# Weighted-value matmuls of an attention slot dealt out between feed-forward matmuls (slots 9 to 31)

## The chip, the cores and the metric

The kernel runs on one core of one Trainium2 chip. The metric is the device time of one execution in microseconds (us). The engines are written as the profile writes them: PE (TensorE, matmuls), PEld (its weight loads), DVE (VectorE), ACT (ScalarE), POOL (GpSimd), SP (SyncE). Each engine works through its own list of instructions in order.

## The reference

Attention with a relative position bias feeds a bilinear feed-forward layer. Cut to what matters:

```python
# q, k, v: (8, 8, 576, 64): batch, heads, positions, head size
scores = scale * q @ k.T + bias            # bias depends on head and on |i - j|
attn   = exp(scores - max) ; attn = attn / (sum(attn) + 1e-9)
x      = (attn @ v)  -> (8 * 576, 512)     # the heads of a position side by side
out    = ((x @ w_a) * (x @ w_b)) @ w_out   # w_a, w_b: 512 x 1536; w_out: 1536 x 512
```

"Weighted values" are the product attn @ v. The kernel divides by the sum of a row only after that product: v carries a column of ones, so the same matmuls give the sums.

## The kernel before

**Pairs and slots.** Two heads of one batch make a pair p, and there are 32 pairs, four to a batch. After a written-out opening (pairs 0 to 7 and the first feed-forward work), a loop over s = 8 to 32 (from line 868) treats one pair in each "slot" s: it computes the scores and exponentials of pair s, the weighted values of pair s - 1, and a fixed quota of feed-forward work on tokens that were finished long before. The slot is a Python list of steps, `steps`, and the order of the steps is the order in which the instructions stand on every engine: the kernel places them by hand (`manual_schedule`). The framework adds the semaphores, one for each read of something that another engine writes and for each buffer that is used again.

**Scores.** `qk(s, 0)` and `qk(s, 2)` are two pairs of score tiles of 128 x 1024 (line 415), each from four 512-column matmuls on half the rows of the array. `ex` (ACT, line 439) takes the exponential into a bfloat16 tile `at`, out of a pool of ten. `mul` (DVE, line 444) multiplies it by the bias table. The last 64 positions have tiles of their own: `qk(s, 2)` adds eight 64-column matmuls into the tiles `trb` and `qr` (line 424), `qk_tail` makes `qkt`, `ex_tail` and `mul_tail` (line 531) finish the tile `att`. `qr` is a tile of the pool `ps_av`, which has one buffer.

**Weighted values.** `av(p, jqs)` is `av_mm` and then `av_norm`. `av_mm(p, (0, 1, 2))` takes the same single buffer of `ps_av` and puts 27 matmuls into it: for each of three blocks of 128 positions one of 130 columns (line 568) and eight of 65 columns (line 578). `av_mm(p, (3, 4))` is the second block of 14: one of 130 and eight of 65, then five of 130 columns for the last 64 positions (lines 568 and 572). Each of them has a weight load of its own, since the attention tile is the stationary operand. `av_norm` runs on DVE: the reciprocal of the sums (line 589), a multiplication into the tile `XG` (line 591), and for the second block two small ones (line 596). After the second block `t_x` sends two DMA transposes from SP, which bring `XG` into `xn`, the feed-forward input (lines 604 and 607).

**Feed-forward.** A unit is four 512-column matmuls: `ff_a` (tile pa, then a copy by ACT, line 649), `ff_b` (tile pb, then DVE's product `g`, line 652), both through `ff_in` (line 642), or a third of an output tile po (`ff_o_mm`, line 679). A chunk of 512 tokens is 24 units of pa and pb in turn and then 12 of po. pa, pb and po share two PSUM buffers. In the list of steps each "unit" stands for one such unit, nine to a slot.

**Order of a slot before.** With U for a unit, a slot with s % 4 of 1, 2 or 3 reads:

```
qk(s,0) ex0 | U ex1 AV(0,1,2) U mul0 U mul1 | v_next qk(s,2) ex2 ex_rows U ex3 U mul2 mul_rows |
AV(3,4) t_x U | U mul3 | qk_tail ex_tail U U mul_tail
```

In slots with s % 4 = 0 ("fourth slots": 12, 16, 20, 24 and 28 among those that the change touches) the part AV(3,4) t_x U and one more U stand before v_next and qk(s,2), so that the last pair of a batch is ready for the next slot's feed-forward. Slot 8 has no weighted values. Slot 32 has no new pair: it starts with AV(0,1,2) and goes on with units.

Of the kernel before, what the change touches and what calls it, by code (L numbers as in the profile page):

```python
# [13 lines left out]
def kernel(  # L14
# [11 lines left out]
    nc = tc.nc  # L26
    FP32 = mybir.dt.float32
# [4 lines left out]
    B, H, S, Dh = 8, 8, 576, 64  # L32
# [18 lines left out]
    ps_av = ctx.enter_context(tc.tile_pool(name="ps_av", bufs=1, space=bass.MemoryType.PSUM))  # L51
# [192 lines left out]
    def warm_up(n, dst=None):  # L244
        for _ in range(n):
# [7 lines left out]
                     start=True, stop=True)  # L253
# [154 lines left out]
    def qk(p, t0, ts=None):  # L408
        qT, kT, _ = operands(p)
        st[p].setdefault("at", [None] * NM)  # L410
        for t in ts or (t0, t0 + 1):
            ps = ps_sc.tile([128, 2, 512], FP32, tag="sc", name=f"qk{p}_{t}")
            for hh in range(2):
                r = slice(64 * hh, 64 * hh + 64)
                nc.tensor.matmul(out=ps[:, hh, :], lhsT=kT[r, t, :], rhs=qT[r, :, :],  # L415
                                 start=True, stop=True)
            st[p]["ps", t] = ps
        if shared(p) and t0 == 2:
            z = operands(p)[2]
            rows = (trb.bitcast(FP32), ps_av.tile([128, 512], FP32, tag="av", name=f"qr{p}"))  # L420
            for t in range(NM):
                for hh in range(2):
                    r = slice(64 * hh, 64 * hh + 64)
                    nc.tensor.matmul(out=rows[hh][:, ST * t:ST * t + ST], lhsT=kT[r, t, :],  # L424
                                     rhs=z[r, 0, ST * hh:ST * hh + ST], start=True, stop=True)
            st[p]["rows"] = rows

    def ex_rows(p):
        st[p]["att"] = at = att[p % 2]
        for hh in (1, 0):  # L430
            nc.scalar.activation(
                out=at[:, 0:512].rearrange("p (t h c) -> p h t c", h=2, t=NM)[:, hh, :, :],
                in_=st[p]["rows"][hh][:, 0:256].rearrange("p (t c) -> p t c", t=NM),
                func=ACTF.Exp, scale=scale)

    def ex(p, t):
        ps = st[p]["ps", t]
        at = atp.tile([128, 2, SM], BF16, tag="at", name=f"at{p}_{t}")
        nc.scalar.activation(out=at[:, :, :], in_=ps[:, :, :], func=ACTF.Exp, scale=scale)  # L439
        st[p]["at"][t] = at  # L440

    def mul(p, t):
        at, w = st[p]["at"][t], W_sb[p % 4]
        nc.vector.tensor_tensor(out=at[:, :, :], in0=at[:, :, :],  # L444
                                in1=w[:, :, S - 1 + t:S - 1 + t - SM:-1], op=MULT)
# [95 lines left out]
    def weights(p, t, hh, jq):  # L541
        if p >= 4:
            return st[p]["at"][t][:, hh, 128 * jq:128 * jq + 128]
        o = 256 * (t % 2) + 128 * (jq % 2)
        return st[p]["at", jq // 2, t // 2][:, hh, o:o + 128]

    def weights_last(p, t):
        return st[p]["att"][:, 2 * ST * t:2 * ST * t + 2 * ST]

    def weights_tail(p, jq):  # L550
        if jq == 4:
            o = 512 + main_tail(p)
            return st[p]["att"][:, o:o + 2 * ST]
        if p < 4 and jq < 2:
            return atk[:, p, 128 * jq:128 * jq + 128]
        o = 512 + 128 * (jq if p >= 4 else jq - 2)
        return st[p]["att"][:, o:o + 128]
# [2 lines left out]
        av_mm(p, jqs)  # L560
        av_norm(p, jqs)

    def av_mm(p, jqs, pool=None, tag="av"):
        b, hp = divmod(p, 4)
        i = b % 2
        pav = (pool or ps_av).tile([128, 3, 2, Dh + 1], FP32, tag=tag, name=f"av{p}_{jqs[0]}")
        for slot, jq in enumerate(jqs):
            nc.tensor.matmul(out=pav[:, slot, :, :], lhsT=weights_tail(p, jq),  # L568
                             rhs=vt[i][:, :, hp, :], start=True, stop=True)
            if jq == 4:  # L570
                for t in range(NM):
                    nc.tensor.matmul(out=pav[:, slot, :, :], lhsT=weights_last(p, t),  # L572
                                     rhs=vm[i][:, 2 * hp:2 * hp + 2, t, :], start=False,
                                     stop=True, skip_group_check=True)
                continue
            for hh in range(2):
                for t in range(NM):
                    nc.tensor.matmul(out=pav[:, slot, hh, :], lhsT=weights(p, t, hh, jq),  # L578
                                     rhs=vm[i][:, 2 * hp + hh, t, :], start=False,
                                     stop=True, skip_group_check=True)  # L580
        st[p]["pav", jqs[0]] = pav

    def av_norm(p, jqs):
        pav = st[p]["pav", jqs[0]]
# [15 lines left out]
    def t_x(p, jqs=range(5), eng=None):  # L600
        b, hp = divmod(p, 4)
        c0 = SM * B + ST * b
        if 4 <= p < NP - 1:
            nc.sync.dma_start_transpose(
                out=xn_sb[hp][:, SM * b:SM * b + SM].rearrange("d (j c) -> d j c", j=4),
                in_=XG[p % 2][:, 0:4, :, :].rearrange("p j h d -> p (j h d)"))
            nc.sync.dma_start_transpose(
                out=xn_sb[hp][:, c0:c0 + ST],
                in_=XG[p % 2][0:ST, 4, :, :].rearrange("p h d -> p (h d)"))
            return  # L610
        tr_x(p, jqs)
        copy_x(p, jqs, eng)
# [16 lines left out]


    ff = {"late": False, "n": 0}

    def ff_bank(name):
        ff["n"] += 1
# [4 lines left out]
    def ff_in(w, kind, c, df, lo, n):  # L639
        ps = ff_bank(f"{kind}{c}_{df}_{lo}")  # L640
        for mc in range(NMC):
            nc.tensor.matmul(out=ps[:, 0:n], lhsT=w[df // 4][:, mc, 128 * (df % 4):128 * (df % 4) + 128],  # L642
                             rhs=xn_sb[mc][:, 512 * c + lo:512 * c + lo + n],
                             start=(mc == 0), stop=(mc == NMC - 1))
        ff[kind, df, lo] = ps

    def ff_ha(c, df, lo, n):
# [26 lines left out]
    def ff_o_mm(c, tt, part):  # L674
        if part == 0:
            ff["po", tt] = ff_bank(f"po{c}_{tt}")
        po = ff["po", tt]
        for df in range(4 * part, 4 * part + 4):
            nc.tensor.matmul(out=po[:, :], lhsT=g_sb[df][:, 128 * tt:128 * tt + 128],  # L679
                             rhs=wo_sb[:, df, :], start=(df == 0), stop=(df == NDF - 1))  # L680

    def ff_o_out(c, tt):
        ob = ob_last if (c, tt) == (0, 2) else wrk.tile([128, DM], FP32, tag="ob", name=f"ob{c}_{tt}")
# [43 lines left out]
    def v_next(s):  # L727
        if s % 4 == 0:
            v_in(s // 4, 0, 4)
        if s % 4 == 2:  # L730
            v_in(s // 4, 4, 8)
# [136 lines left out]
    for s in range(8, NP + 1):  # L868
        new = s < NP
        U = "unit"  # L870
        A = lambda *jq: (lambda: av(s - 1, jq) if s > 8 else None)
        steps = []
        if new:
            steps += [lambda: (qk(s, 0), ex(s, 0))]
        if new:
            head = [U, lambda: ex(s, 1), A(0, 1, 2), U, lambda: mul(s, 0), U,
                    lambda: mul(s, 1)]
            late = [A(3, 4), lambda: t_x(s - 1), U]
            if s == 8:
                late = [U]  # L880
            pair = [lambda: v_next(s), lambda: (qk(s, 2), ex(s, 2), ex_rows(s)), U,
                    lambda: ex(s, 3), U, lambda: mul(s, 2), lambda: mul_rows(s)]
            tail = [lambda: (qk_tail(s), ex_tail(s)), U, U, lambda: mul_tail(s)]
            if s % 4 == 0:
                steps += head + late + [U] + pair + [lambda: mul(s, 3)] + tail
            else:
                steps += head + pair + late + [U, lambda: mul(s, 3)] + tail
        else:
            ff["late"] = True
            steps += [A(0, 1, 2), U, U, U, A(3, 4), lambda: t_x(s - 1, (0, 1, 2)), U, U, U,  # L890
                      lambda: t_x(s - 1, (3, 4)), U, U, U]
        b = s // 4 + 1
        if s % 4 == 2 and b < B:
            t_half(b, 0)
        if s % 4 == 0 and 2 <= b - 1 < B:
            t_half(b - 1, 1)
        if s % 4 == 1 and 2 <= b < B:
            load_vt(b)
        for bb in range(3, B):
            for g in range(2):  # L900
                if s == load_slot[bb] + (2 - (bb < 5)) * g:
                    load_half(bb, g)
        quota = 9
        seen, put = 0, 0
        nu = sum(1 for x in steps if x is U)
        for x in steps:
            if x is U:
                seen += 1
                n = (quota * seen + nu - 1) // nu - put
                put_units(n)  # L910
                put += n
            else:
                x()
# [31 lines left out]
```

## Time and profile before

| | us |
|---|---|
| runs (three) | 412.92, 413.51, 413.57; median 413.51 |
| span of the profiled execution | 412.1 |
| median of the runs less that span | 1.4 |
| PE busy | 401.5 |
| ACT busy | 252.0 |
| DVE busy | 240.6 |
| POOL busy | 131.4 |
| PE busy between 85 and 336 (slots 8 to 31) | 248.87 of 251.00 |

The span runs from the first to the last instruction of the profiled execution; a run's time holds what lies around it as well. "Busy" sums the time in which an engine had an instruction under way. Matmuls overlap at their ends, so what a matmul costs is read from the distance between the starts of two that follow each other, not from its length. The view of waits tells which engine stood idle, before which line, and what ended that; the timeline lists instructions with start and length, like ones merged (x4 means four). A slot begins with its first score matmul; slot 12 begins at 116.18 us, slot 14 at 138.19 and slot 15 at 149.20.

### The profile page before, as it was taken

How to read it: one execution, taken by the hardware profiler on the slowest of the kernel's cores; microseconds unless marked ns; L12 is line 12 of the kernel's file. 1: busy time of each engine (PE TensorE's matmuls, PEld its weight loads, DVE VectorE, ACT ScalarE, POOL GpSimd, SP SyncE). 2: the span in 40 equal slices, each digit the busy share in tenths (PEclk: the TensorE clock that was granted, in tenths of full speed). 3: DMA queues.
4: the chain of work that ended last, by engine and by line, in shares of the span. 5: the costliest groups of instructions: out<-in, count | busy, mean ns of one | idle time of the engine just before them, and what ended most of it. 6: DMA issues, size and time to landing. Idle time of an engine off the chain costs nothing.

```text
span 412.1 us, 8718 instructions
## 1 busy us (share of the span) xinstructions
PE 401.5 (97%) x3420; PEld 209.6 (51%) x3471; DVE 240.6 (58%) x568; ACT 252.0 (61%) x386; POOL 131.4 (32%) x188
## 2 busy tenths in 40 slices
PE   7999999999999999999999999999999999999996
PEld 3476656455554555455445555555445454444443
DVE  4799997366755765476646764567547652421320
ACT  5898992577748665667557765767476642322321
POOL 5966466887029400960069004300000000000000
PEclk9999999999999999999999999999999999999999
DMA  9999999999969924994199908960520012002004
GB/s 152 185 204 197 206 137 148 166 184 131 91 127 157 141 40 91 151 127 94 35 159 150 120 17 136 117 92 17 117 67 17 16 40 78 0 5 98 2 2 102
DMA packets 135962, 42.36 MB, mean 103 GB/s; under 512 B 113544, under 2 KB 131176, under 8 KB 135920
## 3 DMA queue, kind: packets, MB, share of 16 engines
q0 software_dynamic: 81120, 19.88, 54.9%
q1 hardware_dynamic: 49456, 12.61, 19.9%
q10 hardware_dynamic: 5344, 9.31, 7.1%
q8 instruction: 27, 0.44, 0.5%
q14 instruction: 15, 0.12, 0.1%
HBM read 39.23 MB, written 9.45 MB: 118 GB/s over the span
## 4 chain that ended last, share of the span: by engine, by line
PE 95%; DMA 1%; ACT 1%; issue 1%; DVE 0%; ACTq 0%; SPq 0%
PE pb L642 23%; PE pa L642 23%; PE po L679 22%; PE av L578 8%; PE qk L415 7%; PE av L568 2%; PE av L572 2%; PE qkh L455 1%; PE qkt L488 1%; DMA xn<-in_k_dram 1%; PE trb L330 1%; PE trb L424 1%; PE trk L330 1%; ACT ath L461 0%; PE qkt L494 0%
## 5 line engine op out<-in xcount | busy, mean ns | idle before, releaser
L439 ACT ACTIVATE at<-qk 128x1024 bf16<-128x1024 f32 x112 | 113.4, 1029 | 27.4 <-DMA out_dram<-ob 10.3
L652 DVE TENSOR_TENSOR g<-pb,ha 128x512 bf16<-128x512 f32 (+1 forms) x114 | 75.6, 663 | 74.8 <-PE pb L642 58.5
L642 PE MATMUL pb<-xn,wb 128*128 128x512 bf16 (+1 forms) x440 | 111.1, 368 | 0.8
L642 PE MATMUL pa<-xn,wa 128*128 128x512 bf16 (+1 forms) x440 | 110.8, 368 | 0.7
L649 ACT ACTIVATE ha<-pa 128x512 f32<-128x512 f32 (+1 forms) x114 | 66.3, 581 | 67.6 <-PE pa L642 63.8
L679 PE MATMUL po<-wo,g 128*128 128x512 bf16 x403 | 95.5, 379 | 0.8
L444 DVE TENSOR_TENSOR at<-at,W 128x1024 bf16<-128x1024 bf16 x112 | 75.0, 685 | 22.4 <-ACT at L439 22.3
L642 PEld LDWEIGHTS <-wa 128*128 128x128 bf16 x456 | 41.2, 98 | 46.6 <-issue 6.8
L642 PEld LDWEIGHTS <-wb 128*128 128x128 bf16 x456 | 40.6, 98 | 42.9 <-issue 4.7
L679 PEld LDWEIGHTS <-g 128*128 128x128 bf16 x420 | 38.8, 98 | 44.9 <-issue 2.5
L684 ACT ACTIVATE ob<-po 128x512 f32<-128x512 f32 x34 | 20.4, 600 | 40.2 <-PE po L679 30.1
L578 PE MATMUL av<-vm,at 128*128 128x65 bf16 x896 | 41.2, 193 | 0.0
L578 PEld LDWEIGHTS <-at 128*128 128x128 bf16 x896 | 37.4, 97 | 6.1
L174 POOL DMA_DIRECT2D vt<-in_v_dram x12 | 7.4, 622 | 101.9 <-PE av L572 101.1
L136 POOL DMA_DIRECT2D qn<-in_q_dram x48 | 36.6, 825 | 9.2 <-PE trb L501 6.9
L589 DVE RECIPROCAL rc<-av 128x6 f32<-128x6 f32 (+1 forms) x64 | 11.9, 186 | 45.7 <-PE av L578 41.1
L145 POOL DMA_DIRECT2D kn<-in_k_dram x48 | 36.2, 800 | 2.6 <-DMA qn<-in_q_dram 1.6
L568 PE MATMUL av<-vt,att 128*128 128x130 bf16 x152 | 33.6, 221 | 0.2
L415 PE MATMUL qk<-QB,KB 64*128 64x512 bf16 x192 | 29.1, 381 | 0.3
L591 DVE TENSOR_TENSOR XG<-av,rc 128x384 bf16<-128x384 f32 (+2 forms) x64 | 27.2, 425 | 2.2
L515 ACT ACTIVATE att<-qkt 128x640 bf16<-128x640 f32 x24 | 16.8, 701 | 13.0 <-PE qkt L489 13.0
L568 PEld LDWEIGHTS <-att 128*128 128x128 bf16 x152 | 14.9, 98 | 6.4
(105 smaller groups left out, 322.8 us busy)
## 6 DMA issues: line engine op xcount, KB each, us to landing
out_dram<-ob ACTq DMA_DIRECT2D x31, 256.0 KB, 2.9
vn<-in_v_dram POOLq DMA_DIRECT2D x16, 256.0 KB, 5.7
kn<-in_k_dram POOLq DMA_DIRECT2D x48, 64.0 KB, 4.9
qn<-in_q_dram POOLq DMA_DIRECT2D x48, 64.0 KB, 4.1
wa<-in_moe_w_a_dram POOLq DMA_DIRECT2D x3, 512.0 KB, 8.9
wb<-in_moe_w_b_dram POOLq DMA_DIRECT2D x3, 512.0 KB, 8.3
wo<-in_moe_w_out_dram POOLq DMA_DIRECT2D x1, 1536.0 KB, 15.7
xn<-XG SPq DMA_TRANSPOSE x52, 3.5
```

The source lines that it names most:

```text
L136: nc.gpsimd.dma_start(out=by_tile(qn[b % 2])[:, h0 // 4, t, :, :], in_=q[b, h0:h1, 128 * t:128 * t + 128, :].transpose([1, 0, 2]))
L145: nc.gpsimd.dma_start(out=by_tile(kn[b % 2])[:, h0 // 4, t, :, :], in_=k[b, h0:h1, t:SM:NM, :].transpose([1, 0, 2]))
L415: nc.tensor.matmul(out=ps[:, hh, :], lhsT=kT[r, t, :], rhs=qT[r, :, :], start=True, stop=True)
L439: nc.scalar.activation(out=at[:, :, :], in_=ps[:, :, :], func=ACTF.Exp, scale=scale)
L444: nc.vector.tensor_tensor(out=at[:, :, :], in0=at[:, :, :], in1=w[:, :, S - 1 + t:S - 1 + t - SM:-1], op=MULT)
L568: nc.tensor.matmul(out=pav[:, slot, :, :], lhsT=weights_tail(p, jq), rhs=vt[i][:, :, hp, :], start=True, stop=True)
L578: nc.tensor.matmul(out=pav[:, slot, hh, :], lhsT=weights(p, t, hh, jq), rhs=vm[i][:, 2 * hp + hh, t, :], start=False, stop=True, skip_grou ...
L591: nc.vector.tensor_tensor(out=xg[:, jqs[0]:jqs[0] + m, :, :], in0=pav[:, 0:m, :, 0:Dh], in1=rc[:, 0:m, :].unsqueeze(3).to_broadcast([128, ...
L642: nc.tensor.matmul(out=ps[:, 0:n], lhsT=w[df // 4][:, mc, 128 * (df % 4):128 * (df % 4) + 128], rhs=xn_sb[mc][:, 512 * c + lo:512 * c + lo ...
L649: nc.scalar.activation(out=ha[:, 0:n], in_=ff["pa", df, lo][:, 0:n], func=ACTF.Copy)
L652: nc.vector.tensor_tensor(out=g_sb[df][:, lo:lo + n], in0=ff["pb", df, lo][:, 0:n], in1=ff["ha", df, lo][:, 0:n], op=MULT)
L679: nc.tensor.matmul(out=po[:, :], lhsT=g_sb[df][:, 128 * tt:128 * tt + 128], rhs=wo_sb[:, df, :], start=(df == 0), stop=(df == NDF - 1))
```

## The change

`av_mm` becomes `av_list`, which returns the same matmuls as a list of calls; the PSUM tile is taken when the first is called. A queue, `feed`, holds such a list, followed by `av_norm` and, for the second block, by `t_x`. After each 512-column matmul of `ff_in` and `ff_o_mm` the function `feed_some` calls as many items of the queue as its rate allows: the number of items plus one, divided by a number of matmuls that is given. For the first block that is (28 + 1) / 12, or / 8 in a fourth slot; for the second (16 + 1) / 16, or / 8. `feed_all` empties the queue.

In the loop the first block is queued ahead of the slot's first unit. The second is queued where AV(3,4) stood (in a fourth slot, after two units). `feed_all` stands before v_next and qk(s,2), and before `mul_tail` at the slot's end. In most slots this makes the order: qk(s,0); three units with the first block dealt out behind their twelve matmuls; qk(s,2) and two units; four units with the second block behind their sixteen matmuls, and qk_tail among them. The opening and slot 32 keep their blocks whole.

```diff
-    def av_mm(p, jqs, pool=None, tag="av"):
+    def av_list(p, jqs, pool=None, tag="av"):
...
+        def mm(slot, hh, start, lhsT, rhs):
+            def put():
+                if ("pav", jqs[0]) not in st[p]:
+                    st[p]["pav", jqs[0]] = (pool or ps_av).tile([128, 3, 2, Dh + 1], FP32, tag=tag,
+                                                                name=f"av{p}_{jqs[0]}")
...
+                nc.tensor.matmul(out=out, lhsT=lhsT, rhs=rhs, start=start, stop=True,
+                                 skip_group_check=not start)
+            return put
...
+    def av_mm(p, jqs, *pool):
+        for put in av_list(p, jqs, *pool):
+            put()
...
+    feed = {"q": [], "rate": 0.0, "due": 0.0}
+
+    def feed_some():
+        feed["due"] += feed["rate"]
+        while feed["q"] and feed["due"] >= 1:
+            feed["due"] -= 1
+            feed["q"].pop(0)()
+        if not feed["q"]:
+            feed["due"] = 0.0
+
+    def feed_all():
+        while feed["q"]:
+            feed["q"].pop(0)()
+
+    def feed_av(p, jqs, matmuls, then=None):
+        feed_all()
+        feed["q"] = [*av_list(p, jqs), lambda: av_norm(p, jqs), *([then] if then else [])]
+        feed["rate"], feed["due"] = (len(feed["q"]) + 1) / matmuls, 0.0
...
+            feed_some()
...
-            head = [U, lambda: ex(s, 1), A(0, 1, 2), U, lambda: mul(s, 0), U,
+            q4 = s % 4 == 0
+            first = [] if s == 8 else [lambda: feed_av(s - 1, (0, 1, 2), 8 if q4 else 12)]
+            rest = [] if s == 8 else [lambda: feed_av(s - 1, (3, 4), 8 if q4 else 16, lambda: t_x(s - 1))]
+            head = [*first, U, lambda: ex(s, 1), U, lambda: mul(s, 0), *(rest if q4 else []), U,
                     lambda: mul(s, 1)]
-            late = [A(3, 4), lambda: t_x(s - 1), U]
-            if s == 8:
-                late = [U]
-            pair = [lambda: v_next(s), lambda: (qk(s, 2), ex(s, 2), ex_rows(s)), U,
+            late = [*([] if q4 else rest), U]
+            pair = [feed_all, lambda: v_next(s), lambda: (qk(s, 2), ex(s, 2), ex_rows(s)), U,
                     lambda: ex(s, 3), U, lambda: mul(s, 2), lambda: mul_rows(s)]
-            tail = [lambda: (qk_tail(s), ex_tail(s)), U, U, lambda: mul_tail(s)]
+            tail = [lambda: (qk_tail(s), ex_tail(s)), U, U, feed_all, lambda: mul_tail(s)]
```

More of the change, by code (lines that the diff above doesn't have):

```diff
@@ L561, in av @@
         av_norm(p, jqs)
-    def av_mm(p, jqs, pool=None, tag="av"):
+    def av_list(p, jqs, pool=None, tag="av"):
         b, hp = divmod(p, 4)
         i = b % 2
-        pav = (pool or ps_av).tile([128, 3, 2, Dh + 1], FP32, tag=tag, name=f"av{p}_{jqs[0]}")
+        def mm(slot, hh, start, lhsT, rhs):
[3 more added lines that the diff above has]
+                                                                name=f"av{p}_{jqs[0]}")
+                out = st[p]["pav", jqs[0]][:, slot, :, :] if hh is None else st[p]["pav", jqs[0]][:, slot, hh, :]
+                nc.tensor.matmul(out=out, lhsT=lhsT, rhs=rhs, start=start, stop=True,
+                                 skip_group_check=not start)
+            return put
+        todo = []
         for slot, jq in enumerate(jqs):
-            nc.tensor.matmul(out=pav[:, slot, :, :], lhsT=weights_tail(p, jq),
-                             rhs=vt[i][:, :, hp, :], start=True, stop=True)
+            todo.append(mm(slot, None, True, weights_tail(p, jq), vt[i][:, :, hp, :]))
             if jq == 4:
                 for t in range(NM):
-                    nc.tensor.matmul(out=pav[:, slot, :, :], lhsT=weights_last(p, t),
-                                     rhs=vm[i][:, 2 * hp:2 * hp + 2, t, :], start=False,
-                                     stop=True, skip_group_check=True)
+                    todo.append(mm(slot, None, False, weights_last(p, t), vm[i][:, 2 * hp:2 * hp + 2, t, :]))
                 continue
@@ L577, in av_mm @@
                 for t in range(NM):
[L578 to L581, printed above, removed]
+                    todo.append(mm(slot, hh, False, weights(p, t, hh, jq), vm[i][:, 2 * hp + hh, t, :]))
+        return todo
+    def av_mm(p, jqs, *pool):
+        for put in av_list(p, jqs, *pool):
+            put()
     def av_norm(p, jqs):
@@ L680, in ff_o_mm @@
                              rhs=wo_sb[:, df, :], start=(df == 0), stop=(df == NDF - 1))
+            feed_some()
     def ff_o_out(c, tt):
```

## The prediction

> **What bounds the kernel now.** I read the page first (engine shares, the slices, the chain that ended last), then the waits of PE alone, then the timeline of two steady slots.
>
> ```profile
> span 412.1 us, 8718 instructions
> ...
> PE 401.5 (97%) x3420; PEld 209.6 (51%) x3471; DVE 240.6 (58%) x568; ACT 252.0 (61%) x386; POOL 131.4 (32%) x188
> ...
> PEclk9999999999999999999999999999999999999999
> ...
> PE 95%; DMA 1%; ACT 1%; issue 1%; DVE 0%; ACTq 0%; SPq 0%
> ```
>
> PE is busy 97% of the span, carries 95% of the chain, and its granted clock is full. The waits of PE list these as the longest:
>
> ```profile
> PE warm L246 <- DVE zero_sb L236: 1.2, 1, 1.2
> PE trk L330 <- DVE kn L322: 1.0, 1, 1.0
> PE qkt L494 <- ACT ath L461: 0.5, 1, 0.5
> ```
>
> All of them lie in the first 25 us. In slots 8 to 31 PE waits for nobody, so a slot costs what its matmuls cost: 11.01 us (slot 14 begins at 138.19, slot 15 at 149.20). Two things follow. Only shorter matmul spacing can make those slots faster; and any wait that the change puts on PE there is paid in full, since PE has no idle time to pay it from.
>
> **The change.** It removes and adds no arithmetic. In slots 9 to 31 (23 slots) the 41 weighted-value matmuls of a slot, which stood in two blocks (27, then 14), are dealt out behind 512-column matmuls: the 27 over 12 of them and the 14 over 16; in slots 12, 16, 20, 24, 28 ("fourth slots") over 8 and 8. With each block's end moves its normalisation on DVE, and with the second also the two DMA transposes on SP's queue.
>
> **1. What hiding weight loads can give.** The timeline of PE in slot 14 (start, length, operation); the first and the later lines show what a block costs.
>
> ```profile
> 138.73 1.04 PE L642 MATMUL pb<-xn,wb 128*128 128x512 bf16 x4
> ...
> 140.24 0.22 PE L568 MATMUL av<-vt,att 128*128 128x130 bf16 x1
> 140.30 0.42 PE L578 MATMUL av<-vm,at 128*128 128x65 bf16 x8
> 140.56 1.02 PE L642 MATMUL pa<-xn,wa 128*128 128x512 bf16 x3
> 141.42 1.03 PE L642 MATMUL pb<-xn,wb 128*128 128x512 bf16 x4
> 142.38 0.61 PE L415 MATMUL qk<-QB,KB 64*128 64x512 bf16 x4
> 142.82 0.19 PE L424 MATMUL trb<-ZB,KB 64*128 64x64 bf16 x1
> 142.82 0.19 PE L424 MATMUL qr<-ZB,KB 64*128 64x64 bf16 x1
> ```
>
> A 512-column matmul takes 0.216 us from start to start. Eight of 65 columns take 0.26 us (140.30 to 140.56), 32.5 ns each, where streaming alone would be 65/512 x 216 = 27.4 ns. Single starts in the trace show 29 ns between the first and second 65-column matmul of a run and 32.5 between later ones. So little of a weight load is exposed: 3.3 ns. Dealing out puts more of them first behind a long matmul: in a normal slot 12 groups instead of 3 runs and 8 singles instead of 1 run, 16 x 3.3 = 53 ns; in a fourth slot about 8 x 3.3 = 26 ns. 18 x 0.053 + 5 x 0.026 = **1.1 us gained**. Bounds: nothing, or all 28 that wait now, 28 x 3.3 ns x 23 = 2.1 us. For a loss by mixing there is no sign: the step from 512 columns to av is 216 ns, from av to 512 columns 33 to 34 ns, as inside either block.
>
> The Trainium skill (TensorE: Matmul & The Clock Gate, "Back-to-back issue gap") speaks for a far larger gain: it gives about 81 ns for each pair of weight load and 128-column matmul. By that figure some 24 more hidden loads in a normal slot and 13 in a fourth one, at 81 - 29 = 52 ns, would be an estimated 26 us gained and about 403 us in all. The rows here are 32.5 ns for 65 and 60 ns for 130 columns, and they decide.
>
> **2. What moving the normalisation costs.** The first block's PSUM tile comes from a pool with one buffer, and the score tile qr takes the same buffer. The order of the changed program shows the weight load of qr waiting for DVE's XG multiplication, as before; new is how close they stand. The normalisation on DVE in slot 14 as it is now (start, length, operation, idle time before):
>
> ```profile
> 140.76 0.20 DVE L589 RECIPROCAL rc<-av 128x6 f32<-128x6 f32 x1 [0.19 <-PE av L578]
> 140.99 0.56 DVE L591 TENSOR_TENSOR XG<-av,rc 128x384 bf16<-128x384 f32 x1
> ```
>
> And PE in slot 12, a fourth slot, where the second block follows the first:
>
> ```profile
> 118.29 0.42 PE L578 MATMUL av<-vm,at 128*128 128x65 bf16 x8
> 118.55 1.67 PE L679 MATMUL po<-wo,g 128*128 128x512 bf16 x7
> 120.27 0.22 PE L568 MATMUL av<-vt,att 128*128 128x130 bf16 x1
> ```
>
> The last av of the block starts at 140.30 + 7 x 0.0325 = 140.53. From there: 0.23 to the reciprocal, 0.23 to the multiplication, 0.56 of it, 0.055 from a DVE end to PE (opening: KT's copy ends 7.860, its reader on PE starts 7.915). **Chain: 1.075 us.** It is hidden now: it ends at 141.60 and qr comes at 142.82.
>
> (a) 18 normal slots. After the change the last av stands directly before the second pair of score matmuls. To qr it is 0.033 + 0.096 (141.42 to 142.38 is four matmuls and 0.096) + 0.44 = 0.57 us. PE waits 1.075 - 0.57 = 0.50 us. The other way round: 1.22 us of slack, less eight matmuls of 0.216 = 1.73, is -0.51. In slots with s % 4 of 1 or 3 the second of the three units is pb, and DVE then has its g (0.61 from start to start) and the first at multiplication (0.60) ahead of the reciprocal: g starts 0.49 after the eighth long matmul's start, the reciprocal could so start 1.70 after it, against 1.43 + 0.23 = 1.66 by the av. There it is 0.54. 12 x 0.54 + 6 x 0.50 = **9.5 us**.
>
> (b) 5 fourth slots. Now 1.7 us of po matmuls lie between the two blocks (118.55 to 120.27). After it, the second block's first matmul stands one 512-column matmul behind the first block's last: 0.033 + 0.216 = 0.25. Wait 1.075 - 0.25 = 0.83; 5 x 0.83 = **4.1 us**.
>
> (c) The second block ends one or two long matmuls ahead of the slot's end, and the next slot's first av needs its buffer. Its chain, from the rows at 146.59 to 147.45 in slot 14: 0.26 + 0.21 + 0.20 + 0.45 + 0.055 = 1.17 us. Distance: 0.06 + 2 x 0.216 + 0.096 + 0.54 (score matmuls) + 0.216 = 1.34. Slack 0.17, or 0.07 where a g stands before it on DVE: no wait in 17 slots, but close. Slot 32 has no score matmuls: 0.06 + 2 x 0.216 = 0.49, wait **0.7 us**.
>
> (d) A weight load that waited is no longer hidden. In the opening such loads shift the next matmul by 12 ns (25.20) up to 96 ns (6.73). I take 50 ns: 24 x 0.05 = **1.2 us**, bounds 0.3 and 2.3.
>
> What is queued behind: on PE everything, in order. On DVE the reciprocal now holds up the second at multiplication and, in a third of the slots, a g; that g must end before the second unit after qr, 0.3 us to spare, at no cost. The transposes on SP come up to 4 us later, 3.5 us to landing; their reader is at least some 6 us away (from the sixteenth long matmul of a fourth slot to the fourth of the next slot: 24 x 0.216 and the score matmuls between), and the kn, qn transposes queued behind them are used two slots on: no cost, while that cover holds. The at tiles live longer, but at most eight at once of the pool's ten.
>
> **Sum:** 9.5 + 4.1 + 0.7 + 1.2 - 1.1 = +14.4 us. The span 412.1 becomes 426.5; the runs shown have a median of 413.51, 1.4 us around the span, so 427.9 us.
>
> The clock stays out of it. PE stood 1.0 us before 6.73 and the clock row is full there. The Trainium skill (same page, "A second HAM failure mode: psum-queue depth-cycling") warns that micro-idling between PSUM banks lets the clock gate swing; its window is 3.4 us, my waits are below 0.9, and no row here shows a drop.
>
> **Rivals.**
> - *The waits also bind at slot starts.* If the second chain is 0.25 us later than I have it (a g or mul_tail ahead), (c) gives 17 x 0.15 to 17 x 0.25 more, 2.5 to 4.3 us: about 431 us. For: 0.07 of slack. Against: the DVE rows leave gaps there.
> - *Smaller waits.* If PE can overlap qr's wait with its neighbours (the first trb needs no buffer) or DVE finishes sooner by 0.2 us, 24 x 0.2 = 4.8 us less: about 423 us.
> - *Faster.* If the normalisation is out of PE's way, only the gain is left: 413.5 - 1.1 to - 2.1, about 412 us. It decides from the distance of last av to qr: 0.57 here, it would have to be 1.08, two or three more long matmuls. Against: the order of the program has none there.
> - *No effect*: av spacing does not change and nothing waits, 413.5. Against: the same order.
>
> **How the numbers follow.** Forecast 0.66, slot starts bind 0.18, smaller waits 0.09, faster 0.04, no effect 0.03. A measurement of this kernel tells about 0.2% from no change. Slower holds the first three, 0.93; same 0.03; faster 0.04. Range: the forecast with gain 0 to 2.1, loads 0.3 to 2.3 and waits 0.1 us either way (24 x 0.1 = 2.4) is 424.5 to 431.5; a little more for the neighbours: 423.5 to 432.0.
>
> **What would show it.** In the profile after: PEld L424 <- DVE XG, 18 times about 0.5 us; a weight load of av <- DVE XG, 5 times about 0.85; slots of 11.5 us; 65-column spacing near 31 ns. Wrong it would be if qr starts on time (then the chain is shorter), or if the spacing falls far below 29 ns.

## The result and the profile after

The changed kernel takes 429.48 us (median of four runs, 429.31 to 430.13), the kernel before 413.54 us on the same chip (four runs, 412.92 to 413.87). The ratio is 1.0387, 95% interval 1.0372 to 1.0402: 15.9 us slower. The prediction was 427.9 in a range of 423.5 to 432.0.

The page of the profiled execution after (430.13 us) answers to the first lines shown of before:

```profile
span 428.4 us, 8704 instructions
...
PE 406.9 (95%) x3415; PEld 210.4 (49%) x3471; DVE 239.8 (56%) x568; ACT 254.0 (59%) x386; POOL 132.0 (31%) x188
...
PEclk9999999999999999999999999999999999999999
...
PE 86%; DVE 8%; issue 2%; DMA 1%; ACT 1%; ACTq 1%; SPq 0%; another core or an unknown queue 0%; DVEq 0%
```

The clock row is as full as before and the 3471 weight loads are the same work. What moved is the chain: DVE had 0% of it and now has 8%. (PE's busy time grew too, but overlapping matmul records do not sum to cost. Some records are missing, hence x3415.) The waits of PE after (waited for: us in total, times, longest):

```profile
PE qr L424 <- DVE XG L601: 6.2, 18, 0.4
PE av L573 <- DVE XG L601: 3.3, 5, 0.7
PE warm L246 <- DVE zero_sb L236: 1.2, 1, 1.2
PE trk L330 <- DVE kn L322: 1.0, 1, 1.0
PE av L573 <- ACT ob L714: 0.6, 1, 0.6
```

Two lines of this are new in slots 9 to 31, with exactly the 18 and 5 occurrences that the prediction names. The last line is slot 32. Its named releaser ob ends at 352.47, after the av has started at 352.46, so it cannot have been that; the normalisation of the pair before ends at 352.31 and is what the av waited for. Idle time is counted from the end of the last record, and such ends overlap the following matmul; so the price of each wait is larger than in this view and has to be read from start to start. In slot 14, on PE (start, length, operation, idle before):

```profile
146.14 0.19 PE L573 MATMUL av<-vm,at 128*128 128x65 bf16 x1
146.27 0.61 PE L415 MATMUL qk<-QB,KB 64*128 64x512 bf16 x4
146.71 0.19 PE L424 MATMUL trb<-ZB,KB 64*128 64x64 bf16 x1
147.22 0.20 PE L424 MATMUL qr<-ZB,KB 64*128 64x64 bf16 x1 [0.32 <-DVE XG L601]
```

and on DVE at the same place:

```profile
146.37 0.20 DVE L599 RECIPROCAL rc<-av 128x6 f32<-128x6 f32 x1 [1.05 <-PE av L573]
146.60 0.56 DVE L601 TENSOR_TENSOR XG<-av,rc 128x384 bf16<-128x384 f32 x1
```

The last av starts at 146.14, the reciprocal 0.23 later, the multiplication ends at 147.16, and qr starts 0.06 after that. Without the wait qr would stand beside the first trb, at 146.72: 0.50 us lost. In slot 12, a fourth slot, the second block's first matmul stands one long matmul behind the first block:

```profile
121.78 0.23 PE L573 MATMUL av<-vm,at 128*128 128x65 bf16 x2
121.84 0.38 PE L708 MATMUL po<-wo,g 128*128 128x512 bf16 x1
122.89 0.23 PE L573 MATMUL av<-vt,att 128*128 128x130 bf16 x1 [0.67 <-DVE XG L601]
```

It was due at 121.84 + 0.216 = 122.06 and came at 122.89: 0.83 us.

**A wait that the list does not show.** In odd slots (s % 4 of 1 or 3) PE loses a third piece, too short to open a gap between records. Slot 13 after, on PE, the first two units behind qr and the start of the third:

```profile
136.04 0.81 PE L670 MATMUL pb<-xn,wb 128*128 128x512 bf16 x3 [0.16 <-issue]
136.69 1.03 PE L670 MATMUL pa<-xn,wa 128*128 128x512 bf16 x4
137.70 0.38 PE L670 MATMUL pb<-xn,wb 128*128 128x512 bf16 x1
```

and on DVE the product g that empties the first pb:

```profile
136.96 0.69 DVE L681 TENSOR_TENSOR g<-pb,ha 128x512 bf16<-128x512 f32 x1 [0.82 <-PE pb L670]
```

The four pa matmuls would be over at 136.69 + 4 x 0.216 = 137.55. The next pb uses the PSUM buffer of the pb two units earlier, whose g ends at 136.96 + 0.69 = 137.65; it starts 0.055 later, at 137.70. That is 0.15 us. Before, the same place held the second av block, some 0.6 us of matmuls between pa and pb (slot 13 before, on PE):

```profile
132.90 1.03 PE L642 MATMUL pa<-xn,wa 128*128 128x512 bf16 x4
133.76 0.22 PE L568 MATMUL av<-vt,att 128*128 128x130 bf16 x1
...
134.37 0.81 PE L642 MATMUL pb<-xn,wb 128*128 128x512 bf16 x3
```

and on DVE the g of the first pb ended at 133.17 + 0.69 = 133.86, half a microsecond before the next pb at 134.37:

```profile
133.17 0.69 DVE L652 TENSOR_TENSOR g<-pb,ha 128x512 bf16<-128x512 f32 x1 [0.59 <-PE pb L642]
```

So the whole block covered g as well.

| from start to start, mean, us | before | after | difference | slots |
|---|---|---|---|---|
| slot with s % 4 of 1 or 3 | 11.002 | 11.663 | 0.661 | 12 |
| slot with s % 4 of 2 | 11.010 | 11.479 | 0.469 | 6 |
| fourth slot | 11.008 | 11.820 | 0.812 | 5 |
| slot 32 | | | 0.785 | 1 |

12 x 0.661 + 6 x 0.469 + 5 x 0.812 + 0.785 = 15.6 us. The spans differ by 16.3 us, and the other 0.66 us lies ahead of slot 8 (it begins at 73.72 before, at 74.38 after; the row "85 and 336" of the first table therefore begins in slot 9, which starts at 83.17). The change does not touch that part, and over the profiled executions of all kernels here slot 8 begins anywhere from 72.57 to 74.38. The spans of the other three executions after are 427.5 to 427.8.

### The profile page after: what moved, and what is told of

Its sections match the earlier page's. It is cut to its first block, busy times and chain, and to the rows that moved or that the text cites. A ratio compares the mean times of both kernels' runs of the same rounds, so it can differ in the third digit from the quotient of the medians.

```text
span 428.4 us, 8704 instructions
## 1 busy us (share of the span) xinstructions
PE 406.9 (95%) x3415; PEld 210.4 (49%) x3471; DVE 239.8 (56%) x568; ACT 254.0 (59%) x386; POOL 132.0 (31%) x188
## 4 chain that ended last, share of the span: by engine, by line
PE 86%; DVE 8%; issue 2%; DMA 1%; ACT 1%; ACTq 1%; SPq 0%; another core or an unknown queue 0%; DVEq 0%
PE pb L670 22%; PE po L708 20%; PE pa L670 20%; PE av L573 12%; PE qk L415 5%; DVE XG L601 3%; DVE g L681 2%; DVE at L444 1%; PE qkh L455 1%; PE qkt L488 1%; PE qr L424 1%; DMA xn<-in_k_dram 1%; DVE rc L599 1%; PE trb L330 1%; PE trk L330 1%
## 5 line engine op out<-in xcount | busy, mean ns | idle before, releaser
L670 PE MATMUL pa<-xn,wa 128*128 128x512 bf16 (+1 forms) x437 | 118.8, 367 | 0.3
L670 PE MATMUL pb<-xn,wb 128*128 128x512 bf16 (+1 forms) x438 | 118.2, 367 | 0.5 <-issue 0.3
L708 PE MATMUL po<-wo,g 128*128 128x512 bf16 x403 | 104.2, 379 | 0.5 <-issue 0.2
L573 PE MATMUL av<-vm,at 128*128 128x65 bf16 x896 | 99.2, 194 | 1.4
L444 DVE TENSOR_TENSOR at<-at,W 128x1024 bf16<-128x1024 bf16 x112 | 75.9, 685 | 19.7 <-ACT at L439 19.6
L573 PEld LDWEIGHTS <-at 128*128 128x128 bf16 x896 | 65.5, 97 | 29.6
L670 PEld LDWEIGHTS <-wa 128*128 128x128 bf16 x456 | 42.7, 98 | 38.2 <-issue 6.8
L670 PEld LDWEIGHTS <-wb 128*128 128x128 bf16 x456 | 42.4, 98 | 38.7 <-issue 4.7
L573 PEld LDWEIGHTS <-att 128*128 128x128 bf16 x280 | 25.4, 97 | 12.7 <-DVE XG L601 4.9
```

The costliest lines, as they stand in the source:

```text
L444: nc.vector.tensor_tensor(out=at[:, :, :], in0=at[:, :, :], in1=w[:, :, S - 1 + t:S - 1 + t - SM:-1], op=MULT)
L573: nc.tensor.matmul(out=out, lhsT=lhsT, rhs=rhs, start=start, stop=True, skip_group_check=not start)
```

## The experiments

My theory, W: the loss is waits alone, since blocks whose end stood far from the next user of a buffer now end close to it. The main rival, M: dealing out costs by itself (mixing short and long matmuls, exposed weight loads, alternating PSUM buffers), and the waits are what such a stream shows. Edits are against the changed kernel unless said, and shortened: `first:` and `rest:` name the call that the list holds, ex1 stands for `lambda: ex(s, 1)` and so on, and lines without effect on the order are left out. Times in brackets are those of the kernel before in the same session.

**1. The first block four long matmuls sooner.**

```diff
-  first: feed_av(s - 1, (0, 1, 2), 8 if q4 else 12)
+  first: feed_av(s - 1, (0, 1, 2), 4 if q4 else 8)
```

> The changed kernel, with the first block dealt out over 8 long matmuls instead of 12, and over 4 instead of 8 in the fourth slots; 27 av still go in between. Four long matmuls (0.86 us) then stand between the block's last av and what needs its buffer. Theory W (PE waits for the normalisation on DVE): the 18 waits of qr (0.51 to 0.54 us, 9.5 us) and the 5 of the second block's first av (0.83, 4.1 us) go; what stays is a wait of 0.15 us on g in 12 slots (1.8), slot 32 (0.8) and a gain near 0.9: about 415.5 us. Theory M (dealing out itself costs PE, some 15.5 us over about 560 changes between av and long matmuls): 22 of 26 groups of a slot stay, about 427 us. Theory L (DVE is too late as a whole): the waits shrink by less than half, about 424 us.

418.00 us [413.84], ratio 1.0101 (1.0085 to 1.0116). No wait on XG is left before qr or av, which speaks for W, but 2.5 us more than W's number remain. (L, that DVE as a whole is too late, had expected 424.) Slots are 11.206 (odd), 11.13 (s % 4 of 2) and 10.986 (fourth). The g wait of 0.15 is still there in the odd slots, and other waits are new. In slots with s % 4 of 2 a pa waits 0.16 us for ACT's copy ha of the pa before (in slot 14 the copy ends at 145.27, pa starts at 145.32). In the odd slots it is DVE; in slot 13:

```profile
130.80 0.20 DVE L599 RECIPROCAL rc<-av 128x6 f32<-128x6 f32 x1 [3.03 <-PE av L573]
131.03 0.56 DVE L601 TENSOR_TENSOR XG<-av,rc 128x384 bf16<-128x384 f32 x1
131.51 0.68 DVE L681 TENSOR_TENSOR g<-pb,ha 128x512 bf16<-128x512 f32 x1
```

The block now ends inside a pb unit, so its normalisation is issued ahead of that unit's own g. That g starts 0.69 us late, and the pb behind qr waits 0.10 us for it. One slot (25) is 0.5 us longer still: its pa waited for a DMA transpose of XG. Together, 12 x 0.10 + 6 x 0.16 + 0.5 = 2.7 us, which covers the 2.5.

**2. Nothing dealt out, but the first block late.** The kernel before, with the whole block moved behind the third unit in slots with s % 4 of 1, 2 or 3:

```diff
-  head = [U, ex1, A(0, 1, 2), U, mul0, U, mul1]
+  head = [U, ex1, U, mul0, U, A(0, 1, 2), mul1]     # s % 4 != 0
```

> The kernel before, nothing dealt out; only in slots whose number is no multiple of 4 the whole first block stands behind the third unit instead of the first, directly ahead of the second pair of score matmuls. Theory W: qr waits 0.50 to 0.54 us in 18 slots, 9.2 us, and in the 6 slots that start with pb the third unit waits about 0.15 for g (0.9): about 423.5 us. Theory M: no mixing, so no cost: 413.5 us.

426.54 us [413.84], ratio 1.0303 (1.0288 to 1.0319). Not one av is mixed in here, and the same wait appears in the same 18 slots (waits of PE):

```profile
PE qr L424 <- DVE XG L591: 5.8, 18, 0.3
PE pa L642 <- ACT ha L649: 1.5, 6, 0.2
```

From start to start it is 0.505 us in all 18, 9.1 us. The other 3.4 us are at the units that the block used to separate: 0.41 us in the slots with s % 4 of 1, where pa waits for ACT's copy ha of the pa before (not foreseen: 6 x 0.41 = 2.5 of the 3.0 us by which W's number is too low), and 0.15 in those of 2, where pb waits for g. M falls as the main cause: where the block ends sets the price, mixed or not.

**3. Only the second block dealt out**, the first whole where it was:

```diff
-  head = [*first, U, ex1, U, mul0, *(rest if q4 else []), U, mul1]
+  head = [U, ex1, A(0, 1, 2), U, mul0, *(rest if q4 else []), U, mul1]
```

> The first block whole and where it was before, the second dealt out as in the changed kernel. Theory W: no wait of qr; the wait on g (12 slots, 0.15 us, 1.8 us) and slot 32 (0.8) stay, gain 0.4: about 415.7 us, with the wait in front of the first pb behind qr's unit pair in slots with s % 4 of 1 or 3. Theory M: 14 of 26 groups stay, about 421 us.

419.01 us [413.84], ratio 1.0118 (1.0091 to 1.0146), between the two numbers; the slots decide. No qr wait. The g wait of 0.153 stands in the odd slots, and 0.07 more where the pa or po of the next unit waits for ACT's copy ha (in slot 13 the copy ends at 135.71, pa starts at 135.77); one of 0.157 stands between pb and pa in those with s % 4 of 2, slot 32 waits 0.8, and slots 17 and 25 waited for a transpose (0.1 and 0.5 us). That is 12 x 0.22 + 6 x 0.157 + 0.8 + 0.6 = 5.0 us, and the kernel is 5.2 slower: W had missed several of these waits, but no cost is left for M.

**4 and 5. The second block one unit sooner** (behind the first unit after qr), with the edit of experiment 1 (4) and alone (5):

```diff
-  late = [*([] if q4 else rest), U]
+  late = [U]
-  pair = [..., U, ex3, U, mul2, mul_rows]
+  pair = [..., U, ex3, *([] if q4 else rest), U, mul2, mul_rows]
```

> As the kernel with the first block over 8 (4 in fourth slots), and in the other slots the second block dealt out from the second unit behind qr on, one unit sooner, so that av stand between the two units that were 0.15 us apart from g's end, and four long matmuls stand between the block's end and the slot's. Theory W: all waits go (12 x 0.15 and slot 32 as well), and the gain of the hidden weight loads is left, 0.7 to 1.0 us: 412.5 to 413.0 us, 0.2% faster than before. Theory M: about 427 us. If the wait on g has another cause than the lacking av between the units, about 414.5.

415.49 us [413.84] (eight runs), ratio 1.0040 (1.0025 to 1.0055): above W's number by 2.5 to 3 and above the third case by 1.0. The 0.15 us and slot 32's wait are gone. The odd slots (11.165) keep the 0.10 us of experiment 1 and get 0.115 us at the second block's first av, which uses the buffer of qr and is now so near to it that ACT has not read qr yet.

> The changed kernel, with only the second block of the normal slots dealt out one unit sooner, from the second unit behind qr on. Theory W, as it stands now: the 12 waits of 0.15 us on g go, because av stand again between the two units, and slot 32 no longer waits (0.8); the 18 waits of qr and the 5 of 0.83 us stay: 2.6 us less than the changed kernel, about 426.9 us, with slots of 11.51 (s % 4 of 1 or 3), 11.48 (2) and 11.82 us (0). Theory M (mixing costs, no matter where): 429.5 us as the changed kernel. If the 0.15 us are not due to the lacking av, slots stay at 11.66 us and only slot 32 gains: 428.7.

426.99 us [413.67], ratio 1.0321 (1.0296 to 1.0345). Slots 11.513, 11.479 and 11.82: as expected to 0.003. That isolates the unforeseen wait: 12 x 0.15 us, together with slot 32.

**6. Every wait seen so far taken out**: first block sooner and never ending inside a pb unit, second block as in 4 but begun one long matmul later (`due` is the value that the queue's counter starts from).

```diff
+  first: feed_av(s - 1, (0, 1, 2), 8 if s % 4 == 2 else 4)
+  rest:  feed_av(s - 1, (3, 4), 8 if q4 else 16, t_x, due=0.0 if q4 else -1.0)   # placed as in 4
```

> Both blocks still dealt out, but so that every wait seen up to now has its cover back: the first block over 4 long matmuls (8 where the first unit is pb, so that g of a pb never queues behind the normalisation), the second from one long matmul later than in the kernel of 415.5 us, so that ACT has read qr by then. Theory W: slots of 10.98 to 11.01 us, nothing left but the gain of 10 to 40 ns a slot: 413.2 to 413.8 us, no more than 0.2% from before. Theory M: a fixed price for each change between av and long matmul would leave it near 424 us.

416.12 us [413.67], ratio 1.0053 (1.0032 to 1.0074): a miss, 2.3 us above. The waits had moved. In the odd slots the pa or po of the fourth unit behind qr waits 0.10 us for ACT's copy ha (in slot 13 the copy ends at 135.48, pa starts at 135.53). And slots with s % 4 of 2 lose 0.13 us at their start; 12 x 0.10 + 6 x 0.13 = 2.0 us. DVE at the end of slot 13:

```profile
137.86 0.18 DVE L599 RECIPROCAL rc<-av 128x4 f32<-128x4 f32 x1 [0.90 <-PE av L573]
138.08 0.29 DVE L601 TENSOR_TENSOR XG<-av,rc 128x128 bf16<-128x128 f32 x1
138.29 0.45 DVE L606 TENSOR_TENSOR XG<-av,rc 64x64 bf16<-64x64 f32 x2
138.76 0.69 DVE L681 TENSOR_TENSOR g<-pb,ha 128x512 bf16<-128x512 f32 x1
```

The second normalisation ends inside a pb unit here and stands ahead of its g, as the first did in experiment 1; g ends at 139.45, and the next slot's pb starts at 139.51.

**7. Dealt out in the fourth slots alone**, the other slots with whole blocks:

```diff
+  if not q4:
+      head = [U, ex1, A(0, 1, 2), U, mul0, U, mul1]
+      late = [A(3, 4), t_x, U]
```

> Dealt out only in slots 12, 16, 20, 24 and 28; the other slots as before. Theory W: five waits of 0.83 us of the second block's first av, each fourth slot 11.82 us, the others 11.00 to 11.01: 4.1 us over the kernel before, about 417.8 us. Theory M: 5 of 23 slots mix: about 417 us as well, but then with no wait in the fourth slots and wider spacing in them.

417.66 us (one run) [413.67]. The fourth slots take 11.823, the others 11.00 to 11.01. Term (b) stands alone: 5 x 0.82 = 4.1 us.

**8. The first block over 11 long matmuls instead of 12**, which adds one long matmul, 0.216 us, between last av and qr:

```diff
-  first: feed_av(s - 1, (0, 1, 2), 8 if q4 else 12)
+  first: feed_av(s - 1, (0, 1, 2), 8 if q4 else 11)
```

> The changed kernel with the first block dealt out over 11 long matmuls instead of 12 in the normal slots: one long matmul (0.216 us) more between its last av and qr. Theory W: qr's wait falls by the same, from 0.505 to about 0.29 us (s % 4 of 2) and from 0.54 to 0.33 or somewhat more where DVE is behind (1, 3): 18 x 0.21 = 3.8 us less, about 425.7 us. Theory M or L: nothing that one matmul more would take away, 429 us.

429.35 us (one run) [413.67], 3.7 above the expectation. With s % 4 of 2 the wait fell from 0.505 to 0.290, as expected. In the odd slots it rose from 0.541 to 0.600. PE and DVE in slot 13:

```profile
133.88 0.19 PE L573 MATMUL av<-vm,at 128*128 128x65 bf16 x1
...
134.66 0.19 PE L424 MATMUL trb<-ZB,KB 64*128 64x64 bf16 x1
135.26 0.20 PE L424 MATMUL qr<-ZB,KB 64*128 64x64 bf16 x1 [0.41 <-DVE XG L601]
```

```profile
133.22 0.69 DVE L681 TENSOR_TENSOR g<-pb,ha 128x512 bf16<-128x512 f32 x1 [2.79 <-PE pb L670]
133.83 0.68 DVE L444 TENSOR_TENSOR at<-at,W 128x1024 bf16<-128x1024 bf16 x1
134.43 0.19 DVE L599 RECIPROCAL rc<-av 128x6 f32<-128x6 f32 x1
```

The av would let the reciprocal start at 133.88 + 0.23 = 134.11; it starts at 134.43, directly behind g and the multiplication of at. The prediction had seen these two bounds 0.04 us apart; moving one of them alone changes nothing. The other even went the wrong way, since more av stand before the eighth long matmul and g waits for that.

**9. As 6, with the second block out of the pb units too**, over 12 long matmuls in the odd slots:

```diff
-  rest:  feed_av(s - 1, (3, 4), 8 if q4 else 16, t_x, due=0.0 if q4 else -1.0)
+  rest:  feed_av(s - 1, (3, 4), 8 if q4 else 12 if s % 2 else 16, t_x, due=0.0 if q4 else -1.0)
```

> Both blocks dealt out as in the kernel of 416.1 us, but in slots with s % 4 of 1 or 3 the second block over 12 long matmuls instead of 16, so that its normalisation is issued behind a pa unit and not inside a pb unit, where it stood ahead of that unit's g on DVE. Theory W: the wait of the next slot's first pb (0.13 us) and the one of 0.07 beside it go; slots of 10.97 to 11.01 us; the sum of all gains of hidden weight loads is then seen without waits, 0.1 to 0.6 us: 413.2 to 413.9 us. Theory M: about 424 us. If the 0.13 us have another cause, 416 us again.

413.79 us (eleven runs) [414.05], ratio 0.9991 (0.9982 to 1.0000). The waits of PE are again those of the opening alone:

```profile
PE warm L246 <- DVE zero_sb L236: 1.2, 1, 1.2
PE trk L330 <- DVE kn L322: 0.8, 1, 0.8
PE trb L330 <- ACT qn L320: 0.7, 1, 0.7
```

Start to start, 0.035 us is left at a pa in the slots with s % 4 of 2. Slots 10.990, 11.008 and 10.987: 12 x 0.012 + 6 x 0.002 + 5 x 0.021 = 0.26 us less than before. All of the av are still dealt out, over fewer matmuls, and 15.7 us are back. That settles M, and it is also the most that I got from the idea: about 0.3 us, with an interval that reaches to no difference.

**10. Experiment 8 with DVE's bound moved as well**: in odd slots the first multiplication of at stands behind the third unit.

```diff
+  if s % 2 and s > 8:
+      head = [*first, U, ex1, U, U, mul0, mul1]
```

> The kernel with the first block over 11 long matmuls (429.35 us), and in slots with s % 4 of 1 or 3 the bias multiplication mul(s, 0) moved behind the third unit, so that DVE has only one g ahead of the normalisation. Theory L for these slots (g and mul0 on DVE, not the av, set the end of the normalisation there): their wait of qr falls from 0.60 to about 0.29 us, as in the slots with s % 4 of 2; 12 x 0.31 = 3.7 us less, about 425.6 us. If the av set it there too and the 0.60 us came from something else, 429.3 us as before.

425.11 us (one run) [414.05]; the wait before qr is 0.29 in all 18 slots. DVE, slot 13:

```profile
132.10 0.69 DVE L681 TENSOR_TENSOR g<-pb,ha 128x512 bf16<-128x512 f32 x1 [2.79 <-PE pb L670]
132.99 0.20 DVE L599 RECIPROCAL rc<-av 128x6 f32<-128x6 f32 x1 [0.19 <-PE av L573]
133.22 0.56 DVE L601 TENSOR_TENSOR XG<-av,rc 128x384 bf16<-128x384 f32 x1
```

Now the reciprocal waits for the av (0.19 idle before it), and the 0.216 us arrive in the odd slots too. This confirms the cause of experiment 8's miss.

## Why the prediction was right

The direction and the mechanism were right, and one wait was missed: the forecast's time was 1.6 us short of 429.48. That it is no more owes something to luck, since a missed 1.8 us and 0.9 us too much for another term partly cancel. By its own terms:

| term | predicted, us | measured, us |
|---|---|---|
| (a) qr waits in 18 slots | 9.5 | 6 x 0.505 + 12 x 0.541 = 9.5 |
| (b) second block in 5 fourth slots | 4.1 | 5 x 0.83 = 4.2 |
| (c) slot starts; slot 32 | 0; 0.7 | 0; 0.79 |
| (d) weight loads that waited | 1.2 | 0.2 to 0.3 |
| gain of hidden weight loads | -1.1 | -0.9 |
| g before the second unit behind qr | 0 | 12 x 0.152 = 1.8 |
| sum | 14.4 | 15.6 |

- **(a) and (b)** hold to 0.1 us, and experiments 2 and 7 each show one of them without the other. The chain of 1.075 us, taken from the trace of before, was the right length: last av to reciprocal 0.23, 0.23, 0.56, 0.055.
- **(c)** The slots' starts do not wait in the changed kernel, as said, and the slack was as thin as said: between the end of the second normalisation (and 0.055 us to PE) and the next slot's first av lie 0.10 us in 6 and 0.16 to 0.17 us in 11 of the 17 slots; the prediction had 0.07 and 0.17. The wait at slot starts in experiment 6 is another one, of a pb for its buffer.
- **(d)** is the term that was mis-sized. A load that waited delays the next matmul by some 10 ns, the low end that the opening's rows gave (12 ns), not by the 50 I took between 12 and 96: with s % 4 of 2, qr starts 0.505 us late and the unit behind it 0.515. The 96 ns at 6.73 was a misreading: the four pairs of matmuls there follow each other at 0.106 to 0.107 us, the first like the others.
- **The gain** is 0.04 to 0.05 us in a normal slot, where I had 0.053, and 0.02 in a fourth one; this is what is left of the slots' lengths when the waits are taken off, and was not measured by itself. By the figure of the Trainium skill (TensorE: Matmul & The Clock Gate, "Back-to-back issue gap"), about 81 ns for a weight load with a 128-column matmul, it would have been an estimated 26 us. Here such a pair takes 59 to 60 ns with 130 columns, and experiment 9 is 0.26 us faster.
- **The step that failed** is the sentence that a g "must end before the second unit after qr, 0.3 us to spare, at no cost". I had checked the g that the late reciprocal holds up, and that one is in time. I had not checked the next one, which nothing holds up: it is late because the block that stood between its pb and the next user of its buffer is gone. From the last pb start to the release it takes 0.486 + 0.69 + 0.055 = 1.23 us, and PE needs the buffer after 5 x 0.216 = 1.08. Both figures could be read in the profile of before.
- **Around the span** lie 1.75 us, not 1.4: I had set the span of one execution against the median of others, and that execution took 413.87. With the sum's 1.2 this makes the 1.6. The ends of the range were also added up wrongly: its three spreads give 423.6 to 432.5, not 424.5 to 431.5.

The rivals. *Slot starts bind*: no such wait after. *Smaller waits*: qr's wait is not shortened by the trb beside it (146.71 and 147.22 above). *Faster*: its condition was two or three more long matmuls between last av and qr. Experiment 1 has four more and is not faster, because other distances become short; with all of them kept (experiment 9) 0.3 us is left. *No effect*: excluded by the interval. The clock was no part of it: its mean is 0.999 with 23 waits of 0.5 to 0.8 us. The Trainium skill's warning about micro-idling between PSUM banks (same page, "A second HAM failure mode: psum-queue depth-cycling") is not borne out by waits of this length.

What stays open: why the same opening takes up to 1.8 us more in one execution than in another (0.66 us between the two profiles compared here), and why a DMA transpose came late in single slots of experiments 1 and 3.

## What to carry to other kernels

A block of small matmuls on an engine that bounds the kernel may look inefficient and still earn its place: it is the time in which other engines empty the buffers that come next. Before spreading it, list every buffer whose writer and next user it separates (here the score buffer, the feed-forward buffers with DVE's g and ACT's copy, and the tile qr that ACT reads) and compare, for each, the chain from last writer to release with the matmuls that would be left between. When work is dealt out of a queue, look also at where its last item falls: issued inside another unit, it goes ahead of that unit's own instructions on the other engine; and where two bounds lie 0.04 us apart, moving one gives nothing.

## What I had not expected of the hardware

- A hidden weight load seems to be worth 3 ns here: from start to start, a 65-column matmul that stands first behind a longer one takes 29 ns, and one behind another of its kind 32.5. Changing between the two kinds shows no cost: mostly 215 to 216 ns from a long one to av, in blocks and dealt out alike.
- The view of waits gives 0.32 us for qr in slot 14 where 0.50 is lost, and shows nothing at all of the 0.15 us: on PE, whose records overlap, short waits are found by start-to-start distances against 0.216 us.
- The DMA transposes of XG take 2.3 to 7.9 us to land (7.8 at most before). In experiments 1 and 3 one that was issued at 256 to 257 us, in fourth slot 24, took 7.0 and 6.6 us, and pa in slot 25 started 0.5 us late.
